# One transposed order of q's halves, and the other made by two VectorE copies

## Chip, core and metric

The kernel runs on one core of a Trainium2 chip. The metric is the device time of one execution in microseconds; of several runs the median is taken.

## What is computed

An attention layer is followed by two feed-forward layers. The change touches only the attention's preparation of q. Cut to that part, the reference is:

```python
q_pool = q.reshape(B, H, S // 2, 2, D).mean(axis=3)      # B 4, H 8, S 1152, D 64
scores = (1 / np.sqrt(D)) * np.matmul(q_pool, k.transpose(0, 1, 3, 2))
attn = softmax(scores)                                   # 1e-09 added to the sum
x = np.matmul(attn, v)                                   # then moe 1 (h * cos(h)), moe 2 (silu)
```

All inputs are float32.

## The kernel before

TensorE multiplies in float16, so each float32 operand is scaled and split into two float16 halves, hi and lo, and products of halves are summed in PSUM.

**Pairs.** The 32 heads are worked through as 16 pairs. Per pair `pair_loads` (L429) loads q, k and v through SyncE's queue (L433, L436, L442); `pair_prep` (L453) adds the two rows of q that are pooled (POOL, L456), takes absolute maxima (VectorE, `absmax` L126), makes the scales (`scale_steps`, L111 to L119) and splits q (L489 to L495), k (`split`, L446 and L451) and v (`do_v`).

**q and k.** The head dimension is 64, so two halves fit on 128 rows. k's hi and lo are laid side by side and transposed by one DMA (L507): rows 0 to 63 of kT are hi, rows 64 to 127 lo. q is made in two orders, e = 0 as hi over lo and e = 1 as lo over hi. ScalarE casts hi twice (L491), VectorE makes lo once (L492, a fused multiply and subtract) and copies it once (L495), and one DMA transposes both orders, 2 x 9 blocks of 128 x 128 (L497). `tile_scores` (L518) multiplies kT with qT of e = 0 and then of e = 1 into the same PSUM tile, which gives all four products of halves.

**Tiles.** A pair has 9 tiles of 128 query rows. Each tile passes TensorE (scores, L531 or L539), VectorE (scale and minimum out of PSUM, L550, L555), ScalarE (exp, L558; hi cast, L564), POOL (lo, L569), a DMA transpose of 18 blocks (L571) and TensorE again (product with v, L582 and L586). The scores have one PSUM buffer for each of their two column parts. `LAG` keeps four tiles between scores and the product with v.

**Order.** Python generators emit the work: while pair n's tiles run, `prep_then_load` (L957) emits the preparation of pair n + 1 and the loads of pair n + 2, one step every few calls (`slowly`). In the first four pairs the weights of layer 1 are prepared beside this; from the fifth on, matmuls of layer 1 (L667, L722) are mixed in. A scheduler then puts all instructions into one fixed order for each engine's queue by their place in the program, with an offset where `ahead` is used, as they come ready in its own timeline. On the chip each queue runs strictly in that order; an instruction whose input isn't there holds all behind it. All DMAs here, loads and transposes alike, are issued from SyncE's queue (SP).

**Buffers.** qn and kn share the tag "kn" with two buffers (`NB_N`), so qn is always in the one and kn in the other.

Of the kernel before, what the change touches and what calls it, by code (L numbers as in the profile page):

```python
# [12 lines left out]
F16 = mybir.dt.float16  # L13
I32 = mybir.dt.int32
AF = mybir.ActivationFunctionType
ALU = mybir.AluOpType
# [8 lines left out]
END = object()  # L25
P_CH, P_SC, P_EX, P_PV, P_MS, P_MU, P_W, P_PR, P_X = 0, 60, 0, -100, 200, 0, 0, 0, 0
PSH = 15.0
NB_N, NB_SC, NB_H, NB_T, NB_S = 2, 4, 4, 4, 5
X_LAG = 40
W1_BUFS, WT_BUFS = 3, 3  # L30
W1_TABLE = (6, (0, 2, 4, 8, 11), 2)
# [17 lines left out]
def attention_moe_moe_kernel(ctx, tc, q, k, v, w_in1, w_out1, w_in2, w_out2, out):  # L49
# [3 lines left out]
    nc = tc.nc  # L53
    B, H, S, D = q.shape
# [4 lines left out]
    KC = S // 128  # L59
# [24 lines left out]
    def scale_steps(m, pool, res, top, wide=False, apart=False, clean=False, put=lambda ins: ins):  # L84

        n = m.shape[1]
        if wide:  # L90
            w = small.tile([128, 1], F32, name="mw", tag="mw")
            wi, mi = w.bitcast(I32), m.bitcast(I32)
            put(nc.vector.tensor_scalar(
                out=wi, in0=mi, scalar1=3, scalar2=EXP_MASK if clean else 0x3F800000, op0=ALU.logical_shift_left,
                op1=ALU.bitwise_and
            ))
            if not clean:
                nc.vector.scalar_tensor_tensor(
                    out=wi, in0=mi, scalar=1 << 30, in1=wi, op0=ALU.bitwise_and, op1=ALU.bitwise_or
                )  # L100
            m = w
            if apart:
                yield
        if pool is ps_y:
            bc = pool.tile([128, NC, GW], F32, tag="y", name="bm")[:, 0, 0:4]
        else:
            bc = pool.tile([128, 2, GW], F32, tag="h", name="bm")[:, 0, 0:4]
        put(nc.tensor.matmul(bc[:, 0:n], mean, m, start=True, stop=True))
        yield
        s, u = res  # L110
        nc.vector.tensor_scalar(  # L111
            out=u, in0=bc[:, 0:n], scalar1=TINY, scalar2=2.0**(9 - top), op0=ALU.max, op1=ALU.mult
        )

        nc.vector.tensor_scalar(
            out=s.bitcast(I32), in0=u.bitcast(I32), scalar1=EXP_MASK, scalar2=EXP_MASK,
            op0=ALU.bitwise_and, op1=ALU.bitwise_xor,
        )
        nc.vector.tensor_scalar(  # L119
            out=u.bitcast(I32), in0=u.bitcast(I32), scalar1=EXP_MASK, scalar2=None, op0=ALU.bitwise_and  # L120
        )
# [3 lines left out]
    def absmax(out_, in_, axis=AX.X):  # L125
        nc.vector.tensor_reduce(out=out_, in_=in_, axis=axis, op=ALU.max, apply_absolute_value=True)  # L126
# [9 lines left out]
    def early(g, n):  # L136
        while True:
            with ahead(n):
                r = next(g, END)
            if r is END:  # L140
                return
            yield r
# [264 lines left out]
    def att_pools(stack):  # L407
        at = Weights()
        at.p = stack.enter_context(tc.tile_pool(name="att", bufs=2, side="right", reuse_waits="tile"))
        at.src_stack = ExitStack()  # L410
        at.src = at.src_stack.enter_context(tc.tile_pool(name="src", bufs=2, side="right", reuse_waits="tile"))
        at.ps_s = stack.enter_context(tc.tile_pool(name="ps_s", bufs=1, space=PSUM, side="right"))
        at.ps_v = stack.enter_context(tc.tile_pool(name="ps_v", bufs=1, space=PSUM, side="right"))
        return at
# [30 lines left out]
    def split(hi, lo, src, s, on_pool):  # L445
        nc.scalar.activation(out=hi, in_=src, func=AF.Copy, scale=s)  # L446
        if on_pool:
            nc.scalar.activation(out=src, in_=src, func=AF.Copy, scale=s)
            nc.gpsimd.tensor_tensor(out=lo, in0=src, in1=hi, op=ALU.subtract)
        else:  # L450
            nc.vector.scalar_tensor_tensor(out=lo, in0=src, scalar=s, in1=hi, op0=ALU.mult, op1=ALU.subtract)  # L451

    def pair_prep(at, P):  # L453
        NQ = 2 * NT + 1
        qs = P.q[:, :, 0, :]
        nc.gpsimd.tensor_tensor(out=qs, in0=qs, in1=P.q[:, :, 1, :], op=ALU.add)  # L456
        m = small.tile([128, 5], F32, name="pm", tag="pm")
        for i in range(2):
            absmax(m[:, 1 + i:2 + i], P.k[i], AX.XY)
            yield  # L460
        absmax(m[:, 0:1], qs, AX.XY)
        yield
        for i in range(2):
            absmax(m[:, 3 + i:4 + i], P.v[i], AX.XY)
            yield
        m3 = small.tile([128, 3], F32, name="pm3", tag="pm3")
        nc.vector.tensor_copy(m3[:, 0:1], m[:, 0:1])
        nc.vector.tensor_reduce(
            out=m3[:, 1:3], in_=m[:, 1:5].rearrange("p (a b) -> p a b", b=2), axis=AX.X, op=ALU.max
        )  # L470
        s = small.tile([128, 3], F32, name="ps_", tag="ps_", bufs=3)
        u = small.tile([128, 3], F32, name="pu_", tag="pu_", bufs=3)
        yield from early(scale_steps(m3, ps_h, (s, u), 12), P_CH)
        P.s = s
        P.su = small.tile([128, 1], F32, name="psu", tag="psu", bufs=3)
        nc.vector.tensor_scalar(
            out=P.su, in0=u[:, 0:1], scalar1=u[:, 1:2], scalar2=-0.125 / math.sqrt(D), op0=ALU.mult, op1=ALU.mult
        )
        P.vt = [None] * 2

        def do_v(i):

            P.vt[i] = vt = at.p.tile([128, KC, 2, D + 1], F16, tag="vt", name="vt", bufs=VT_BUFS)
            nc.gpsimd.memset(vt[:, :, 0, D:D + 1], 1.0)
            nc.gpsimd.memset(vt[:, :, 1, D:D + 1], 0.0)
            split(vt[:, :, 0, 0:D], vt[:, :, 1, 0:D], P.v[i], s[:, 2:3], P.on_pool >= 2)


        qn = at.src.tile([128, 2, NQ, 2, D], F16, tag="kn", name="qn", bufs=NB_N)  # L489
        for e in range(2):  # L490
            nc.scalar.activation(out=qn[:, e, :, e, :], in_=qs, func=AF.Copy, scale=s[:, 0:1])  # L491
        nc.vector.scalar_tensor_tensor(  # L492
            out=qn[:, 0, :, 1, :], in0=qs, scalar=s[:, 0:1], in1=qn[:, 0, :, 0, :], op0=ALU.mult, op1=ALU.subtract
        )
        nc.vector.tensor_copy(qn[:, 1, :, 0, :], qn[:, 0, :, 1, :])  # L495
        qT = at.p.tile([128, 2, NQ, 128], F16, tag="qT", name="qT", bufs=2)
        nc.sync.dma_start_transpose(  # L497
            out=qT.rearrange("p e n k -> p (e n) k"), in_=qn.rearrange("p e n s d -> p (e n s d)")
        )
        P.qT = [qT[:, e] for e in range(2)]  # L500
        yield
        kn = at.src.tile([128, 2, KC, 2, D], F16, tag="kn", name="kn", bufs=NB_N)
        for i in range(2):
            split(kn[:, i, :, 0, :], kn[:, i, :, 1, :], P.k[i], s[:, 1:2], P.on_pool >= 1)
            yield
        kT = at.p.tile([128, 2, KC, 128], F16, tag="kT", name="kT", bufs=2)
        nc.sync.dma_start_transpose(  # L507
            out=kT.rearrange("p i c k -> p (i c) k"), in_=kn.rearrange("p i c s d -> p (i c s d)")
        )
        P.kT = [kT[:, i].rearrange("p c k -> p (c k)") for i in range(2)]  # L510
        yield
        for i in range(2):
            do_v(i)
            yield
# [348 lines left out]
    if True:  # L863
# [6 lines left out]
        at = att_pools(att_stack)  # L870
# [69 lines left out]
        for n in range(2):  # L940
            P[n] = pair_new(at, *pairs[n])
            run_all(pair_loads(P[n]))
            if n == 0:
                wg = layer1_weight_steps(W1, (w_in1, w_out1), wst, lambda: ps_y, nc.sync, W1_BUFS, WT_BUFS, *W1_TABLE)
                next(wg)
                run_all(pair_prep(at, P[0]))
                next(wg)
# [9 lines left out]
        def prep_then_load(n):  # L957
            late = int(n > NP)
            yield from early(slowly(pair_prep(at, P[n]), PREP_PACE[late]), P_PR)
            if n + 1 < len(pairs):  # L960
                P[n + 1] = pair_new(at, *pairs[n + 1])
                yield from slowly(pair_loads(P[n + 1]), LD_PACE[late])
# [290 lines left out]
```

## Time and profile before

| | |
|---|---|
| median of 3 runs | 1365.03 us (1364.72 to 1366.87) |
| the profiled execution's own time | 1363.93 us |
| its span, first to last instruction | 1362.1 us |
| mean granted TensorE clock | 0.925 of full speed |
| busy TensorE, VectorE, ScalarE, POOL | 1139.0, 1039.7, 870.9, 620.3 us |
| DMA queue q1, share of 16 engines' span | 65.8% |
| DMA transposes: hl, q, k, x, x rest | 144, 16, 16, 8, 2 |

Attention runs until about 836 us and overlaps with layer 1 from about 257 us on; the rest is layers 1 and 2. "Busy" is the time with an instruction in work, and a wait is put down to whatever came last. SP's rows give the time for which its queue was issuing a DMA; "to landing" is counted from the start of the issue to the last byte.

### The profile page before, as it was taken

Reading aid. Unit: us, or ns where it says so; the run is one execution under the profiler, and the core shown is the slowest. Engines: PE = TensorE matmul, PEld = TensorE weight load, DVE = VectorE, ACT = ScalarE, POOL = GpSimd, SP = SyncE. Lnnn points to the kernel's source line nnn. Section 1 sums busy time; section 2 is a strip of 40 time slices with the busy share of each in tenths; the row PEclk is TensorE's granted clock in tenths of the full one; section 3 lists DMA queues with packets and bytes.
Section 4 is the critical chain, followed back from the end, with each engine's and each line's share of the span. In section 5 each row is a group of like instructions: output and inputs, shape, how many; then the busy total and the mean of one; then the engine's idle time right before and its main releaser. Section 6 shows DMA issues by size and latency. Waiting matters only on the chain. (4 is left out here: it accounts for less than half of the span.)

```text
span 1362.1 us, 26442 instructions
## 1 busy us (share of the span) xinstructions
PE 1139.0 (84%) x10668; PEld 915.3 (67%) x10668; DVE 1039.7 (76%) x1927; ACT 870.9 (64%) x1061; POOL 620.3 (46%) x352
## 2 busy tenths in 40 slices
PE   2565465788988777889898899989999999999998
PEld 1343243576666556666676678778788888888887
DVE  6898888789876988888898996886757755444483
ACT  3878787778767777877788774544546633433352
POOL 1656675666556466656556562443667400000000
PEclk9667676889998889999899999999899999999999
DMA  9999999988799999988999965423444000000001
GB/s 290 202 212 226 221 231 183 163 168 166 135 204 177 201 199 198 198 151 186 157 202 188 217 129 109 106 81 71 86 91 112 32 25 32 9 16 17 17 32 32
DMA packets 509594, 186.27 MB, mean 137 GB/s; under 512 B 465952, under 2 KB 484384, under 8 KB 509472
## 3 DMA queue, kind: packets, MB, share of 16 engines
q1 hardware_dynamic: 509472, 184.59, 65.8%
q8 instruction: 83, 1.36, 0.4%
q14 instruction: 39, 0.32, 0.1%
HBM read 66.58 MB, written 9.44 MB: 56 GB/s over the span
## 5 line engine op out<-in xcount | busy, mean ns | idle before, releaser
L569 POOL TENSOR_TENSOR hl<-sc,hl 128x1152 f16<-128x1152 f32 x144 | 367.9, 2565 | 201.2 <-ACT hl L564 105.9
L531 PE MATMUL sp<-kT,qT 128*128 128x512 f16 (+1 forms) x768 | 189.4, 366 | 92.7 <-DVE sc L550 70.8
L550 DVE TENSOR_SCALAR_CACHE_REDUCE sc<-sp,psu 128x512 f32<-128x512 f32 (+1 forms) x288 | 228.9, 807 | 49.6 <-PE sp L531 46.2
L667 PEld LDWEIGHTS <-ih 128*128 128x128 f16 x2304 | 225.5, 99 | 42.9 <-issue 12.4
L558 ACT ACTIVATE sc<-sc,nb 128x1152 f32<-128x1152 f32 x144 | 179.8, 1250 | 114.4 <-DVE nb L555 77.8
L582 PE MATMUL pv<-vt,hlT 128*128 128x130 f16 (+1 forms) x1440 | 195.1, 237 | 65.9 <-DMA hlT<-hl 58.3
L582 PEld LDWEIGHTS <-hlT 128*128 128x128 f16 (+1 forms) x1440 | 146.4, 110 | 96.1 <-DMA hlT<-hl 73.4
L667 PE MATMUL h<-ys,ih 128*128 128x256 f16 x1152 | 195.5, 274 | 4.1 <-ACT gs L683 4.1
L667 PE MATMUL h<-xT,ih 128*128 128x256 f16 x1024 | 184.9, 275 | 3.2 <-DMA xT<-xn 3.1
L586 PE MATMUL pv<-vt,hlT 128*128 128x65 f16 (+1 forms) x1440 | 186.3, 207 | 0.0
L531 PEld LDWEIGHTS <-qT 128*128 128x128 f16 x768 | 76.9, 108 | 156.9 <-issue 104.2
L564 ACT ACTIVATE hl<-sc 128x1152 f16<-128x1152 f32 x144 | 164.6, 1153 | 14.5 <-DMA xT<-xn 9.7
L722 PE MATMUL y<-gh,oh 128*128 128x256 f16 x576 | 162.0, 281 | 7.1 <-ACT y L731 7.1
L722 PE MATMUL y<-gl,oh 128*128 128x256 f16 x576 | 161.8, 281 | 2.9 <-POOL gl L711 2.9
L722 PE MATMUL y<-gh,ol 128*128 128x256 f16 x576 | 161.8, 281 | 0.0
L836 PEld LDWEIGHTS <-op 128*128 128x128 f16 x1512 | 147.9, 98 | 18.0 <-issue 0.6
L667 PE MATMUL h<-ys,il 128*128 128x256 f16 x576 | 157.7, 274 | 0.0
L586 PEld LDWEIGHTS <-hlT 128*128 128x128 f16 (+1 forms) x1440 | 143.0, 108 | 15.8 <-issue 6.1
L667 PE MATMUL h<-xT,il 128*128 128x256 f16 x512 | 140.5, 274 | 0.0
L722 PEld LDWEIGHTS <-oh 128*128 128x128 f16 x1152 | 114.8, 102 | 28.1 <-issue 9.4
L711 POOL TENSOR_TENSOR gl<-tt,gh 128x1024 f16<-128x1024 f32 x36 | 92.1, 2559 | 76.4 <-DVE gh L710 71.2
L667 PEld LDWEIGHTS <-il 128*128 128x128 f16 x1152 | 113.7, 99 | 17.8 <-issue 2.9
(310 smaller groups left out, 2039.9 us busy)
## 6 DMA issues: line engine op xcount, KB each, us to landing
wst<-in_moe_w_in_dram SPq DMA_DIRECT2D x16, 1024.0 KB, 5.8
stk<-in_k_dram SPq DMA_DIRECT2D x32, 288.0 KB, 4.0
stv<-in_v_dram SPq DMA_DIRECT2D x32, 288.0 KB, 4.0
stq<-in_q_dram SPq DMA_DIRECT2D x32, 256.0 KB, 3.1
wst<-in_moe_w_out_dram SPq DMA_DIRECT2D x8, 1024.0 KB, 6.2
wst<-in_moe_w_out_dram SPq DMA_DIRECT2D x16, 512.0 KB, 6.0
ydr<-y SPq DMA_DIRECT2D x9, 512.0 KB, 4.3
y32b<-ydr SPq DMA_DIRECT2D x9, 512.0 KB, 3.3
```

The costliest lines, as they stand in the source:

```text
L531: nc.tensor.matmul(sp[:, o - a:o - a + n], P.qT[e][:, t, :], kT[:, o:o + n], start=(e == 0), stop=(e == 1))
L550: nc.vector.tensor_scalar(out=T.sc[:, a:z], in0=sp, scalar1=T.P.su, scalar2=None, op0=ALU.mult, op1=ALU.min, accum_out=mx[:, x:x + 1],)
L558: nc.scalar.activation(out=T.sc, in_=T.sc, func=AF.Exp, scale=-1.0, bias=nb)
L564: nc.scalar.activation(out=hi, in_=T.sc, func=AF.Copy)
L569: nc.gpsimd.tensor_tensor(out=T.hl[:, 1, :], in0=T.sc, in1=T.hl[:, 0, :], op=ALU.subtract)
L582: nc.tensor.matmul(G.pv[r, T.gi], T.hlT[:, 0, c, r], P.vt[i][:, c], start=(c == 0), stop=(c == KC - 1), skip_group_check=True,)
L586: nc.tensor.matmul(G.pv[r, T.gi, 0], T.hlT[:, 1, c, r], P.vt[i][:, c, 0], start=False, stop=(c == KC - 1), skip_group_check=True,)
L667: nc.tensor.matmul(hp, wt[:, c, f * 128:(f + 1) * 128], xt(c), start=(i == 0), stop=(i == 3 * NC - 1), skip_group_check=True,)
L711: nc.gpsimd.tensor_tensor(out=G.gl, in0=t, in1=gh, op=ALU.subtract)
L722: nc.tensor.matmul(blk.y[:, oc, :], wt[:, f, oc * 128:(oc + 1) * 128], gt[:, f % 4, :], start=(f == 0 and e == 0 and oc % 2 == 0), stop=(f ...
L836: nc.tensor.matmul(bank, t[:, e, c, :], wt[:, c, :], start=start, stop=True, skip_group_check=True)
```

## The change

q is split once, hi beside lo, into a buffer of half the size with a tag of its own (one buffer; kn too now has one). The DMA transposes 9 blocks into e = 0 of qT. After the transpose of k has been issued, two VectorE copies write e = 1: rows 0 to 63 from rows 64 to 127 of e = 0, and rows 64 to 127 from rows 0 to 63.

```diff
-        qn = at.src.tile([128, 2, NQ, 2, D], F16, tag="kn", name="qn", bufs=NB_N)
-        for e in range(2):
-            nc.scalar.activation(out=qn[:, e, :, e, :], in_=qs, func=AF.Copy, scale=s[:, 0:1])
-        nc.vector.scalar_tensor_tensor(
-            out=qn[:, 0, :, 1, :], in0=qs, scalar=s[:, 0:1], in1=qn[:, 0, :, 0, :], op0=ALU.mult, op1=ALU.subtract
-        )
-        nc.vector.tensor_copy(qn[:, 1, :, 0, :], qn[:, 0, :, 1, :])
+        qn = at.src.tile([128, NQ, 2, D], F16, tag="qn", name="qn", bufs=1)
+        split(qn[:, :, 0, :], qn[:, :, 1, :], qs, s[:, 0:1], False)
         qT = at.p.tile([128, 2, NQ, 128], F16, tag="qT", name="qT", bufs=2)
-        nc.sync.dma_start_transpose(
-            out=qT.rearrange("p e n k -> p (e n) k"), in_=qn.rearrange("p e n s d -> p (e n s d)")
-        )
+        nc.sync.dma_start_transpose(out=qT[:, 0], in_=qn.rearrange("p n s d -> p (n s d)"))
         P.qT = [qT[:, e] for e in range(2)]
         yield
-        kn = at.src.tile([128, 2, KC, 2, D], F16, tag="kn", name="kn", bufs=NB_N)
+        kn = at.src.tile([128, 2, KC, 2, D], F16, tag="kn", name="kn", bufs=1)
...
         P.kT = [kT[:, i].rearrange("p c k -> p (c k)") for i in range(2)]
+        for x, y in ((slice(0, 64), slice(64, 128)), (slice(64, 128), slice(0, 64))):
+            nc.vector.tensor_copy(qT[x, 1], qT[y, 0])
         yield
```

## Rows read from the trace of the kernel before

**Rows 1.** Busy us of PE, PEld, DVE, ACT, POOL by stage; clock, DMA share, GB/s.
```profile
0.00:267.00 267.00, 144.64 (x1190) 95.44 (x1191) 224.09 (x501) 197.70 (x220) 154.54 (x91) 0.74 1.01 219
267.00:500.00 233.00, 192.28 (x1927) 145.55 (x1925) 193.22 (x384) 174.89 (x208) 138.87 (x74) 0.93 0.94 176
500.00:850.00 350.00, 311.05 (x3137) 239.43 (x3136) 303.80 (x587) 265.08 (x320) 201.40 (x103) 0.98 0.90 174
```

**Rows 2.** Who waited for whom: us in total, times, longest us.
```profile
PE sp L531 <- DVE sc L550: 70.8, 56, 8.6
...
PE pv L582 <- DMA hlT<-hl: 58.3, 30, 5.6
...
DVE pm L126 <- DMA stk<-in_k_dram: 23.4, 13, 6.3
...
DVE pm L126 <- DMA stv<-in_v_dram: 7.0, 5, 2.3
```

**Rows 3.** Timeline of the first pair: start us, us, engine, line; idle before it.
```profile
9.35 0.14 DVE L467 COPY pm<-pm 128x1 f32<-128x1 f32 x1
...
13.43 1.44 ACT L491 ACTIVATE qn<-stq,ps__150 128x576 f16<-128x576 f32 x2
14.24 0.82 DVE L492 SCALAR_TENSOR_TENSOR qn<-stq,ps__150,qn 128x576 f16<-128x576 f32 x1 [1.72 <-ACT qn L491]
...
15.57 1.55 DVE L451 SCALAR_TENSOR_TENSOR kn<-stk,ps__150,kn 128x576 f16<-128x576 f32 x2 [0.15 <-ACT kn L446]
15.67 3.95 SPq L497 DMA_TRANSPOSE qT<-qn  x1
...
19.73 2.75 SPq L507 DMA_TRANSPOSE kT<-kn  x1
...
24.33 2.08 PE L531 MATMUL sp<-kT,qT 128*128 128x512 f16 x6 [12.66 <-DMA kT<-kn]
```

**Rows 4.** Tile qn and tile qT: count, ns shortest, median, longest, starts; time to landing.
```profile
L495 DVE COPY qn<-qn x16: 310/319/781, 15.1 to 748.7; 128x576 f16<-128x576 f16 x16
L497 SPq DMA_TRANSPOSE qT<-qn x16: 2680/3202/5333, 15.7 to 749.1; - x16
...
L492 DVE SCALAR_TENSOR_TENSOR qn<-stq,ps__7680,qn x1: 2924/2924/2924, 653.0 to 653.0; 128x576 f16<-128x576 f32 x1
...
DMA to landing us min/median/max: 4.6/5.8/7.5
```

**Rows 5.** Page, queue q1 (packets, MB, share of 16 DMA engines) and memory totals.
```profile
q1 hardware_dynamic: 509472, 184.59, 65.8%
...
HBM read 66.58 MB, written 9.44 MB: 56 GB/s over the span
```

**Rows 6.** Columns as in rows 1, for a stretch with plain transfers only.
```profile
1000.00:1362.00 362.00, 352.88 (x3213) 314.36 (x3210) 202.86 (x307) 161.42 (x228) 52.86 (x48) 1.00 0.12 35
```

**Rows 7.** Tile xrT, transposes of 8 blocks: ns in SP's queue, us to landing.
```profile
L1097 SPq DMA_TRANSPOSE xrT<-xnr x2: 1355/1491/1627, 876.8 to 879.1; - x2
...
DMA to landing us min/median/max: 3.6/4.3/5.1
```

**Rows 8.** Line L710 by itself: ns shortest, median, longest.
```profile
L710 DVE CAST gh<-tt x36: 665/686/2856, 269.2 to 988.0; 128x1024 f16<-128x1024 f32 x36
```

**Rows 9.** Groups by line and shape: busy us, mean ns, idle before them.
```profile
L569 POOL TENSOR_TENSOR hl<-sc,hl 128x1152 f16<-128x1152 f32 x144 | 367.9, 2565 | 201.2 <-ACT hl L564 105.9 <-issue 45.9 <-DVE sc L550 12.1
...
L710 DVE CAST gh<-tt 128x1024 f16<-128x1024 f32 x36 | 46.0, 1277 | 2.1 <-PE y L722 2.0
```

**Rows 10.** Timeline of the fifth pair, columns as in rows 3.
```profile
217.54 2.21 DVE L492 SCALAR_TENSOR_TENSOR qn<-stq,ps__1893,qn 128x576 f16<-128x576 f32 x1
...
221.30 2.71 SPq L507 DMA_TRANSPOSE kT<-kn  x1
224.10 2.74 SPq L497 DMA_TRANSPOSE qT<-qn  x1
...
228.81 2.99 PE L531 MATMUL sp<-kT,qT 128*128 128x512 f16 x8 [6.07 <-DMA qT<-qn]
```

More of the change, by code (lines that the diff above doesn't have):

```diff
@@ L27 @@
 PSH = 15.0
-NB_N, NB_SC, NB_H, NB_T, NB_S = 2, 4, 4, 4, 5
+NB_SC, NB_H, NB_T, NB_S = 4, 4, 4, 5
 X_LAG = 40
```

## The prediction

> **What bounds the kernel now.** I read the busy times by stage first. Attention fills the time up to about 850 us, and there no engine is full: VectorE is busy 224.1 + 193.2 + 303.8 = 721.1 of 850 us (85%), TensorE 648.0 (76%), while the DMA engines' share is 1.01, 0.94 and 0.90 [rows 1]. In the first stage TensorE works 144.6 of 267 us at a mean granted clock of 0.74, so part of that time at the lower of its two levels (1.2 and 2.4 GHz). After 850 us TensorE is nearly always at work [rows 6] and the change touches nothing. So the change is worth what it does to TensorE's 850 - 648.0 = 202.0 idle us before that. The table of waits comes next: 70.8 us of them end with VectorE's reading of the scores' PSUM (35%), 58.3 us with the landing of a tile's transpose hlT (29%) [rows 2]. I use these two shares as prices: a microsecond added to VectorE's queue costs 0.35, one taken off the chain ScalarE, POOL, DMA that ends in hlT gives back 0.29. That is a choice: a share of waits says what ended them last, not what would end them next.
>
> **What goes: ScalarE.** Two casts in a row take 1.44 us [rows 3], so one takes 0.72; 16 pairs, 11.5 us. It stands in front of the exps and hi casts that feed hlT: 11.5 x 0.29 = 3.3 us.
>
> **What goes: half a transpose.** Queue q1 holds the 16 engines for 65.8% of 1362.1 = 896 us and moves 184.6 MB, of which 76.0 MB are reads and writes of memory [rows 5]. In the stretch without transposes 0.12 x 362 = 43.4 us moved 35 GB/s x 362 us = 12.7 MB, 3.43 us per MB [rows 6]. So plain transfers hold 261 us and the 186 transposes 635 us, an estimated 3.4 us each. Half of q's is 1.7 us a pair, 27.3 us over 16. SP's queue gains as well: q's issue takes 3.20 us at the median [rows 4], 8 blocks take 1.36 to 1.63 [rows 7], so 9 should take some 1.6. The queue behind it is that of the tiles' hlT, so both go to the same wait: 27.3 x 0.29 = 7.9 us. Ends: nothing, if no hlT ever stood behind a q transpose, and the full 1.7 in those pairs where the DMA is full.
>
> **What comes: two VectorE copies a pair.** Each covers 64 rows x 1152 float16. No row shows a copy between halves of the partitions. The nearest is the removed copy, the same type and engine, 576 elements in 310 ns at the shortest [rows 4]; a one-element copy takes 140 ns [rows 3]; so 0.295 ns an element and 0.14 + 0.34 = 0.48 us for 1152. Upper end: the cast from float32, (665 - 140) / 1024 = 0.513 ns an element [rows 8], 0.73 us. Lower end: 0.31, as the removed one. I take 0.48, since type and memory are the same; two are 0.96 us. The removed copy gives back 0.32.
>
> Copies also wait for POOL. The cast L710 takes 0.665 us at the shortest and 1.277 on average, up to 2.86 [rows 8, 9], and q's own subtract 0.82 us alone and 2.92 beside POOL [rows 3, 4]. I take the cast's 1.277 - 0.665 = 0.61 us, once a pair, as the second copy follows the first. The Trainium skill (SBUF — State Buffer, "two separate sides") speaks against the change here: POOL and a VectorE copy use one pair of ports, whoever starts first keeps it for a whole instruction, and the other stands still. By that rule the wait would be POOL's busy share times half of one of its instructions; rows 1 and 9 give 495 / 850 x 2.565 / 2 = 0.75 us, and the sum would be 0.8 us higher. The trace agrees in kind (2.92 for 0.82), and the measured 0.61 stays in the sum.
>
> Together 0.96 + 0.61 - 0.32 = 1.25 us a pair, 20.0 us of VectorE.
>
> **A new wait.** The copies wait for qT's landing, on VectorE's queue, where the next tile's L550 stands behind them, and TensorE's next scores wait for L550. Before, only TensorE waited for qT, usually long after. Landing takes 5.8 us now [rows 4]; for 8 blocks 4.3 [rows 7]. How much of it shows depends on what the fixed order puts between. The nearest row of VectorE waiting for a DMA in its queue is the absolute maxima on k and v: 30.4 us over 64 loads [rows 2], 0.48 us a transfer, or 1.9 us for the four of a pair. I take 0.48 (one transfer), 7.6 us in all; ends 0 and 1.9 us a pair. VectorE in all: 27.6 x 0.35 = 9.7 us lost.
>
> **What moves on SP.** qT's issue no longer waits for the copy L495 and is shorter. In the first pair kT is issued at 19.73, right after q's 3.95 us, though kn was ready at 15.57 + 1.55 = 17.12; the scores start at 24.33 when kT lands [rows 3]. q's issue would start at about 15.1 (14.24 + 0.82) and take 2.0, so kT goes at 17.1, 2.6 us earlier. The copies must be done too: 15.1 + 4.3 = 19.4, two copies 20.4, and a subtract of 0.82 us or the like that VectorE has begun may come first. The scores could start near 22: I take 2.0 us, ends 0 and 2.6. In the fifth pair qn's lo ends at 219.75, kT goes at 221.30 and qT only at 224.10, and TensorE waits 6.07 us for it until 228.81 [rows 10]. Without L495 qT can go first and land near 224; then kT's landing and the copies come last, near 226: I take 2.0 us, ends 0 and 3.5. For the other pairs I count nothing: they are prepared while the tiles of the pair before still run, and that work hides an earlier landing.
>
> The smaller qn in a buffer of its own adds no wait: it is written once in some 50 us, long after its transpose. kn had one buffer in effect before, and has one now.
>
> **The sum.** -2.0 (first pair) -2.0 (fifth) -7.9 (DMA and SP) -3.3 (ScalarE) +9.7 (VectorE) = -5.5 us. The profiled execution took 1363.93 us, of which the span is 1362.1; so it would take 1358.4. The median of the runs stands 1.1 us above the profiled one: 1365.03 - 5.5 = 1359.5 us. With the ends of the copies, of the wait and of the two starts the same sum runs from about 1353 to 1374.
>
> **Rivals.**
> *VectorE stalls behind q's transpose (slower).* Place: the first copy, with L550 behind it. For it: VectorE runs in order, SP's queue lags (qT was issued 4 us after it could have been in the fifth pair, rows 10). Against: VectorE has q's, k's and v's subtracts to do meanwhile. Price: a wait that happened was 30.4 / 18 = 1.69 us [rows 2], and it passes in full, since TensorE's scores wait behind. The rest of the sum without the 7.6 us is -15.2 + 20.0 x 0.35 = -8.2, so it decides from five pairs on; ten of sixteen give +8.7, 1373.7 us; all sixteen 1383.8.
> *POOL holds up both copies (slower).* Each copy waits half a POOL instruction, 1.28 us: 41.0 us in place of 9.8, so +5.4 in all, 1370.4 us. For it: the rows of L710. Against: the removed copy's median of 319 ns.
> *It cancels.* If VectorE's microseconds cost 0.55 instead of 0.35, the 27.6 us are 15.2 and the sum is nought: 1365.0 us. For it: VectorE is the busiest engine up to 267 us, at 84%.
> *The DMA is the bound of the first stage (much faster).* Share 1.01 there: five pairs get the full 1.7 us (8.6), the other eleven 0.29 of it (5.5), 14.1 in place of 7.9, 1353.3 us. Against: hlT's landing ends only 29% of TensorE's idle time.
> That the change doesn't do what it says I leave out: the swapped halves are exactly the other order.
>
> **How the numbers follow.** A measurement of this kernel can tell about 0.2%, 2.7 us, from no change. Forecast 0.38 (of which 0.32 beyond that, 0.06 within), DMA bound 0.12, cancelling 0.18, stall 0.24, POOL 0.08. So faster 0.44, same 0.24, slower 0.32. Cases of both signs hold most of it; the range goes from 1350, below the DMA case, to 1374, and leaves out the stall in more than ten pairs.
>
> **What would show it.** Right: kT's issue near 17 and first scores near 22 us; no wait for qT in the fifth pair; q's issue at 1.5 to 2 us; 32 copies of 0.5 us shortest; fewer waits of L582 for hlT. Wrong: VectorE's wait for qT at the new copies above 1 us a pair, or copies of 0.7 us shortest and 1.3 on average; the DMA share unchanged; TensorE's idle time before 850 us at 202 us or above.

## The result

| | before | changed |
|---|---|---|
| median | 1364.88 us | 1382.45 us |
| lowest to highest of 4 runs | 1363.76 to 1366.87 | 1379.84 to 1387.84 |
| span of the profiled execution | 1362.1 us | 1378.0 us |
| busy VectorE, ScalarE | 1039.7, 870.9 us | 1069.9, 861.2 us |

The change makes the kernel slower: ratio 1.0121, 95% interval 1.0093 to 1.0150, 17.6 us at the medians. 1359.5 was predicted, with 1374 as the upper end. The last product with v starts at 852.7 us in the changed kernel and at 835.8 us before, so nearly all of the loss arises in attention.

The stages of the changed kernel, with the columns of [rows 1]:

```profile
0.00:267.00 267.00, 141.88 (x1155) 91.91 (x1156) 241.73 (x502) 194.55 (x214) 158.28 (x91) 0.76 0.95 211
267.00:500.00 233.00, 194.50 (x1903) 146.15 (x1901) 192.38 (x377) 167.17 (x196) 132.27 (x73) 0.93 0.89 168
500.00:850.00 350.00, 304.21 (x3031) 228.75 (x3030) 310.16 (x578) 260.66 (x313) 205.79 (x104) 0.97 0.87 169
```

The DMA engines' share fell in every stage, as was meant. VectorE's busy time up to 850 us rose by 23.2 us, to 744.3 (88%), and TensorE got 7.4 us less done in the same time. The waits answer to [rows 2]:

```profile
ACT sc L553 <- DVE nb L550: 113.2, 51, 9.5
...
PE sp L526 <- DVE sc L545: 90.7, 69, 5.7
...
PE pv L577 <- DMA hlT<-hl: 30.8, 19, 5.5
```

The first of these lines in the kernel before:

```profile
ACT sc L558 <- DVE nb L555: 77.8, 40, 8.1
```

TensorE's waits for a tile's transpose nearly halved, by 27.5 us. Its waits for VectorE's reading of the scores rose by 19.9 us on the same line, and ScalarE's exps now wait 113.2 us for VectorE's minimum, where they waited 77.8. The waits for a transpose were replaced by waits for VectorE. The lines of q's preparation answer to [rows 4]:

```profile
L505 DVE COPY qT<-qT x32: 454/455/2539, 23.6 to 766.6; 64x1152 f16<-64x1152 f16 x32
L492 SPq DMA_TRANSPOSE qT<-qn x16: 1242/1300/2165, 15.2 to 759.9; - x16
...
DMA to landing us min/median/max: 3.2/3.4/6.3
```

The transpose is cheap as hoped: 1.30 us in SP's queue for 3.20, landing after 3.4 us for 5.8. A copy takes 0.455 us, but up to 2.5. Their group (busy us, mean ns, idle before):

```profile
L505 DVE COPY qT<-qT 64x1152 f16<-64x1152 f16 x32 | 28.5, 890 | 0.7
```

The mean is 0.890, so of the 28.5 us 14.6 are work (32 x 0.455) and 13.9 are not; and VectorE stood idle in front of the copies for only 0.7 us in all, so it didn't wait for q's transpose. The timeline of the second pair shows what the 13.9 us are (start us, us, engine, line):

```profile
46.08 2.13 POOL L226 TENSOR_TENSOR il<-wt,ih 128x1024 f16<-128x1024 f32 x1 [1.69 <-ACT wt L225]
...
46.69 4.39 DVE L505 COPY qT<-qT 64x1152 f16<-64x1152 f16 x2
...
48.17 2.60 POOL L564 TENSOR_TENSOR hl<-sc,hl 128x1152 f16<-128x1152 f32 x1
51.11 0.75 DVE L545 TENSOR_SCALAR_CACHE_REDUCE sc<-sp,psu 128x512 f32<-128x512 f32 x1
...
51.92 0.59 PE L526 MATMUL sp<-kT,qT 128*128 128x512 f16 x1 [4.51 <-DVE sc L545]
```

Two copies take 4.39 us instead of 0.91: POOL is in one instruction when they begin and in the next before they end. L545 of the next tile comes only after them, and TensorE waits 4.51 us for it. In the whole trace the 13.9 us lie in ten of the 32 copies, every one of them beside a POOL instruction; they belong to seven of the 16 pairs, and in three of these both copies waited.

### The profile page after: what moved, and what is told of

It is laid out like the page before. It is cut to its first block, busy times and chain, and to the rows that moved or that the text cites. A ratio compares the mean times of both kernels' runs of the same rounds, so it can differ in the third digit from the quotient of the medians.

```text
span 1378.0 us, 26428 instructions
## 1 busy us (share of the span) xinstructions
PE 1146.5 (83%) x10668; PEld 916.1 (66%) x10668; DVE 1069.9 (78%) x1943; ACT 861.2 (62%) x1045; POOL 627.0 (45%) x352
## 3 DMA queue, kind: packets, MB, share of 16 engines
q1 hardware_dynamic: 491040, 179.87, 62.5%
## 5 line engine op out<-in xcount | busy, mean ns | idle before, releaser
L564 POOL TENSOR_TENSOR hl<-sc,hl 128x1152 f16<-128x1152 f32 x144 | 372.5, 2595 | 205.8 <-ACT hl L559 111.9
L526 PE MATMUL sp<-kT,qT 128*128 128x512 f16 (+1 forms) x768 | 193.2, 365 | 103.4 <-DVE sc L545 90.7
L553 ACT ACTIVATE sc<-sc,nb 128x1152 f32<-128x1152 f32 x144 | 179.8, 1251 | 135.9 <-DVE nb L550 113.2
L662 PEld LDWEIGHTS <-ih 128*128 128x128 f16 x2304 | 226.5, 100 | 44.0 <-issue 11.5
L545 DVE TENSOR_SCALAR_CACHE_REDUCE sc<-sp,psu 128x512 f32<-128x512 f32 (+1 forms) x288 | 228.0, 806 | 34.0 <-PE sp L526 29.7
L577 PE MATMUL pv<-vt,hlT 128*128 128x130 f16 (+1 forms) x1440 | 199.3, 238 | 44.7 <-DMA hlT<-hl 30.8
L662 PE MATMUL h<-xT,ih 128*128 128x256 f16 x1024 | 193.0, 280 | 1.5 <-DMA xT<-xn 1.5
L581 PE MATMUL pv<-vt,hlT 128*128 128x65 f16 (+1 forms) x1440 | 190.5, 208 | 0.0
L662 PE MATMUL h<-xT,il 128*128 128x256 f16 x512 | 143.3, 280 | 0.0
L717 PEld LDWEIGHTS <-oh 128*128 128x128 f16 x1152 | 113.7, 100 | 30.2 <-issue 12.4
```

Of the source, the lines that this page charges most:

```text
L526: nc.tensor.matmul(sp[:, o - a:o - a + n], P.qT[e][:, t, :], kT[:, o:o + n], start=(e == 0), stop=(e == 1))
L545: nc.vector.tensor_scalar(out=T.sc[:, a:z], in0=sp, scalar1=T.P.su, scalar2=None, op0=ALU.mult, op1=ALU.min, accum_out=mx[:, x:x + 1],)
L553: nc.scalar.activation(out=T.sc, in_=T.sc, func=AF.Exp, scale=-1.0, bias=nb)
L564: nc.gpsimd.tensor_tensor(out=T.hl[:, 1, :], in0=T.sc, in1=T.hl[:, 0, :], op=ALU.subtract)
L577: nc.tensor.matmul(G.pv[r, T.gi], T.hlT[:, 0, c, r], P.vt[i][:, c], start=(c == 0), stop=(c == KC - 1), skip_group_check=True,)
L581: nc.tensor.matmul(G.pv[r, T.gi, 0], T.hlT[:, 1, c, r], P.vt[i][:, c, 0], start=False, stop=(c == KC - 1), skip_group_check=True,)
```

## The experiments

The theories, as they came up. **A**: VectorE's added time is the loss, whatever fills it. **B**: the new fixed order of the queues is the loss. **C** and **D**: the wait for q's transpose is (C on the scores' path, D on VectorE's queue). **L**: only standing behind POOL is. **X**: crossing the halves of the partitions is. All times below are medians; the ratio is to the kernel before on the same chip, with its 95% interval, and can differ by some 0.002 from the quotient of the medians. Each kernel gets a fixed order of its own.

### What is the halved transpose worth without the copies?

```diff
-        P.qT = [qT[:, e] for e in range(2)]
+        P.qT = [qT[:, 0], qT[:, 0]]
...
-        for x, y in ((slice(0, 64), slice(64, 128)), (slice(64, 128), slice(0, 64))):
-            nc.vector.tensor_copy(qT[x, 1], qT[y, 0])
```

> The changed kernel without the two VectorE copies; the second matmul of each score reads the same order as the first, so those products are wrong but as many. Theory A (VectorE's load: the copies' 28.5 us on VectorE are the loss, the halved transpose and the cast give a little back): faster than before, 1350 to 1362 us. Theory B (the new fixed order of instructions is the loss, whatever is in it): near the changed kernel, 1374 to 1385. Theory C (the copies make the scores wait for q's transpose and VectorE): as A.

Measured: 1367.92 us, ratio 0.9990 (0.9967 to 1.0014). The half transpose, the cast and L495 are gone, nothing is added, and the time doesn't move. Its waits:

```profile
PE sp L524 <- DVE sc L543: 93.5, 65, 4.8
...
PE pv L575 <- DMA hlT<-hl: 38.0, 27, 5.1
```

Here too the waits for hlT fell (58.3 to 38.0), and those for VectorE rose by as much (70.8 to 93.5), with no work added on VectorE. So, by the interval, the relief is worth between a gain of 4.5 us and a loss of 1.9. The prediction had 11.2 for it, and 4.0 more for the two earlier starts. Unless a loss by order hides a gain here, which this run alone can't exclude (theory B), the whole loss of the change comes with the copies.

### The copies added to the kernel before

```diff
         P.kT = [kT[:, i].rearrange("p c k -> p (c k)") for i in range(2)]
+        for x, y in ((slice(0, 64), slice(64, 128)), (slice(64, 128), slice(0, 64))):
+            nc.vector.tensor_copy(qT[x, 1], qT[y, 0])
```

> The kernel before, all its casts and its whole transpose kept, with the two copies added at the place where the change has them; they write again the values that are there. Theory A: the loss of the change plus what it gave back, 1383 to 1395 us. Theory B: anywhere from 1360 to 1385, not above the changed kernel for a reason. Theory C: at least the changed kernel, 1380 to 1395.

Measured: 1384.45 us, ratio 1.0106 (1.0071 to 1.0140). The copies alone bring the loss of the whole change. Their load isn't the same, though: they take 42.0 us here for 28.5, and VectorE waits 9.2 us for q's transpose in front of them:

```profile
L512 DVE COPY qT<-qT 64x1152 f16<-64x1152 f16 x32 | 42.0, 1313 | 9.7 <-DMA qT<-qn 9.2
```

Within the interval nothing is given back by the halved transpose, as in the run without copies.

### Copies of two columns

In the changed kernel:

```diff
-        P.qT = [qT[:, e] for e in range(2)]
+        P.qT = [qT[:, 0], qT[:, 0]]
...
-            nc.vector.tensor_copy(qT[x, 1], qT[y, 0])
+            nc.vector.tensor_copy(qT[x, 1, 0, 0:2], qT[y, 0, 0, 0:2])
```

> The changed kernel with each copy cut to two columns, so that the wait for the transpose and the place in VectorE's queue stay and the load goes; the second matmul reads the first order as in the run without copies. Theory A: as without copies, within 4 us, 1350 to 1362. Theory B: near the changed kernel, 1374 to 1385. Theory C (the wait itself): 1372 to 1385, while the run without copies is fast.

Measured: 1381.20 us, ratio 1.0094 (1.0057 to 1.0131). And in the kernel before, into a scratch tile:

```diff
         P.kT = [kT[:, i].rearrange("p c k -> p (c k)") for i in range(2)]
+        qx = at.src.tile([128, 2], F16, tag="qx", name="qx", bufs=1)
+        for x, y in ((slice(0, 64), slice(64, 128)), (slice(64, 128), slice(0, 64))):
+            nc.vector.tensor_copy(qx[x], qT[y, 0, 0, 0:2])
```

> The kernel before with two copies of two columns from q's transpose into a scratch tile that nobody reads: a new wait on VectorE and a new fixed order, nearly no load. Theory A: 1362 to 1369 us. Theory B: it differs from before by 5 us or more, either way. Theory C: 1370 or more.

Measured: 1380.60 us, ratio 1.0090 (1.0061 to 1.0119). Both lose nearly as much as the full copies, and theory A as I had put it looked dead. But the load had not gone. The group of the second kernel:

```profile
L513 DVE COPY qx<-qT 64x2 f16<-64x2 f16 x32 | 24.1, 754 | 4.6 <-DMA qT<-qn 4.1
```

A copy of two columns takes 754 ns on average (567 in the other kernel), where 165 is the shortest. The timeline of one pair:

```profile
49.93 2.38 POOL L572 TENSOR_TENSOR hl<-sc,hl 128x1152 f16<-128x1152 f32 x1
50.41 2.12 DVE L513 COPY qx<-qT 64x2 f16<-64x2 f16 x2 [0.91 <-DMA qT<-qn]
```

POOL's instruction ends at 52.31, and two copies that need 0.3 us end at 52.53. So what a copy costs here hardly depends on its length, and these kernels carry 24.1 and 18.1 us on VectorE for 28.5.

### Order alone

Two memsets of two columns at the same place (kernel before):

```diff
         P.kT = [kT[:, i].rearrange("p c k -> p (c k)") for i in range(2)]
+        qx = at.src.tile([128, 2], F16, tag="qx", name="qx", bufs=1)
+        for x in (slice(0, 64), slice(64, 128)):
+            nc.vector.memset(qx[x], 0.0)
```

> The kernel before with two memsets of two columns a pair on VectorE, at the place in the program where the change has its copies: no load to speak of, no wait for q's transpose, but another fixed order (about 1320 of VectorE's 1609 instructions keep their relative place). Theory B (a new fixed order costs about 1%, whatever made it new): 1372 to 1386 us. Theory D (a VectorE instruction that waits for q's transpose is what costs): 1363 to 1370.

Measured: 1369.08 us, ratio 1.0010 (0.9995 to 1.0024).

```diff
-LD_PACE = (2, 2)
+LD_PACE = (2, 3)
```

In the kernel before:

> The kernel before with the loads of later pairs emitted one call later (LD_PACE (2, 3) for (2, 2)): the same instructions, another fixed order from the fifth pair on. Theory B: the order of before is a good draw, this one is 1368 to 1385 us. Theory D: 1362 to 1370.

Measured: 1370.17 us, ratio 1.0013 (0.9997 to 1.0028). In the changed kernel:

> The changed kernel with the same other pace of loads. Theory B: another draw, anywhere from 1365 to 1390 us, at least 4 us from the changed kernel. Theory D: 1378 to 1386, as the changed kernel, since the copies still wait.

Measured: 1384.34 us, ratio 1.0117 (1.0082 to 1.0151). Three new orders, and none moves its kernel by more than 0.2%. That makes theory B unlikely as the cause of 1.2%; an order can still be worth some tenths of a per cent, and one kernel below loses 1% without any work added on VectorE.

### Covering the wait

```diff
-        for x, y in ((slice(0, 64), slice(64, 128)), (slice(64, 128), slice(0, 64))):
-            nc.vector.tensor_copy(qT[x, 1], qT[y, 0])
...
         for i in range(2):
             do_v(i)
             yield
+        for x, y in ((slice(0, 64), slice(64, 128)), (slice(64, 128), slice(0, 64))):
+            nc.vector.tensor_copy(qT[x, 1], qT[y, 0])
+        yield
```

> The changed kernel with the two copies emitted as the last step of a pair's preparation, behind v's split, so that the transpose has long landed. Theory B: 1374 to 1388 us, as the changed kernel. Theory D: the wait is covered, 1362 to 1372.

Measured: 1381.98 us, ratio 1.0094 (1.0069 to 1.0120). The later place gives nothing back, as there was hardly a wait to cover. To take the wait away altogether, the two-column copies read qn, which is there before q's transpose is issued (kernel before):

```diff
+            nc.vector.tensor_copy(qx[x], qn[y, 0, 0, 0, 0:2])
```

> The kernel before with two two-column copies between halves of the partitions a pair, but from qn, which is ready before q's transpose is issued, so nothing waits for the transpose. Theory L: means of 0.4 to 0.8 us for copies of 0.17 at the shortest, 1374 to 1386 us. Theory D: 1363 to 1372.

Measured: 1390.40 us, ratio 1.0159 (1.0125 to 1.0192). No wait for the transpose, and the loss is larger, with 13.6 us of copies on VectorE. The opposite, the wait without a copy:

```diff
+            nc.vector.tensor_reduce(out=qx[x], in_=qT[y, 0, 0, 0:2], axis=AX.X, op=ALU.max)
```

> The run with two-column copies on the kernel before (1380.6 us), with each copy turned into a maximum over the same two columns (a tensor_reduce): the same wait for q's transpose, the same place, an operation whose longest duration in the trace of before shows no wait for POOL. Theory L (a VectorE copy stands still while POOL is in an instruction, however short it is): shortest and mean duration nearly equal, 1363 to 1372 us. Theory D (the wait for q's transpose costs): 1376 to 1386.

Measured: 1375.01 us, ratio 1.0046 (1.0023 to 1.0068), between the two expectations.

```profile
L513 DVE TENSOR_REDUCE qx<-qT x32: 150/152/154, 25.4 to 775.6; 64x1 f16<-64x2 f16 x32
```

The maximum never stands behind POOL (150 to 154 ns, where the copy had 165 to 2417), and VectorE's wait for the transpose was 4.5 us in all. Half a per cent remains that may be this wait or the order. It may also be time of VectorE: its busy time as a whole rose from 1039.7 to 1060.9 us, though the maxima are only 4.9 us of that, so other instructions of it took longer. With the run from qn, theories C and D fall as the main cause.

### Crossing the halves

```diff
+        for x in (slice(0, 64), slice(64, 128)):
+            nc.vector.tensor_copy(qx[x], qT[x, 0, 0, 0:2])
```

> The kernel before with two two-column copies a pair that stay on their own rows (rows 0 to 63 to 0 to 63, 64 to 127 to 64 to 127). Theory L (the copy stands behind POOL): as with crossing rows, mean 0.4 to 0.8 us for 0.17 at the shortest, 1374 to 1386 us. Theory X (crossing the halves of the partitions is what costs): 1363 to 1371.

Measured: 1381.00 us, ratio 1.0095 (1.0069 to 1.0121), mean 735 ns. Copies that stay on their rows cost what crossing ones cost: X falls.

### The copies off VectorE

```diff
-            nc.vector.tensor_copy(qT[x, 1], qT[y, 0])
+            nc.scalar.activation(out=qT[x, 1], in_=qT[y, 0], func=AF.Copy)
```

> The changed kernel with the two copies on ScalarE in place of VectorE, about 1.2 us each, 38 us in all against 11.5 us saved there. Theory L: no wait for POOL; ScalarE has room, 1360 to 1376 us. Theory D (any engine's wait for q's transpose): 1376 to 1390.

Measured: 1369.87 us, ratio 1.0014 (0.9991 to 1.0038), with copies of 1.16 us each, never longer. ScalarE takes 37 us of copies nearly for nothing where VectorE couldn't take 28.5.

```diff
-            nc.vector.tensor_copy(qT[x, 1], qT[y, 0])
+            nc.sync.dma_start(out=qT[x, 1], in_=qT[y, 0])
```

> The changed kernel with the two copies as plain DMAs on SP's queue, 147 KB each: no engine works for them, but SP's queue stands until q's transpose has landed, and half of the saved DMA time is spent again. Theory L: about as without copies, 1358 to 1372 us. Theory D: the tiles' transposes behind them are late, 1374 to 1390.

Measured: 1368.37 us, ratio 0.9996 (0.9978 to 1.0015). With the same two lines moved up behind q's transpose:

> The copies as DMAs on SP's queue, emitted right behind q's transpose instead of behind k's: the waits of TensorE for the copied order (10.2 us in the run with DMAs) go, kT may be later. 1357 to 1368 us if that is what kept that run from gaining; 1366 to 1374 if SP's standing is paid by kT.

Measured: 1367.94 us, ratio 1.0000 (0.9983 to 1.0018). With `nc.scalar.dma_start` at the change's own place:

> The changed kernel with the two copies as plain DMAs from ScalarE's queue, so that SP's queue doesn't stand for the landing; ScalarE may. Could beat the kernel before if the halved transpose is worth anything: 1357 to 1370 us. If it is worth nothing, 1364 to 1370; if ScalarE stands, 1370 or more.

Measured: 1382.11 us, ratio 1.0101 (1.0078 to 1.0123), the one run without work on VectorE that loses 1%. That is above the first two ranges, and the third case isn't what happened: the trace shows no wait of ScalarE for q's transpose. Its DMA issues (us to landing last):

```profile
hlT<-hl SPq DMA_TRANSPOSE x144, 5.3
...
kT<-kn SPq DMA_TRANSPOSE x16, 6.3
```

The tiles' transposes land after 5.3 us (4.9 in the run without copies) and k's after 6.3 (4.8), and ScalarE's queue issues 32 DMAs of 0.5 us. Which of these costs, or whether it is the order, wasn't tried. None of the three forms beats the kernel before.

### Time or POOL

```diff
-            nc.vector.tensor_copy(qT[x, 1], qT[y, 0])
+            nc.vector.tensor_reduce(
+                out=qT[x, 1], in_=qT[y, 0].rearrange("p n (k o) -> p n k o", o=1), axis=AX.X, op=ALU.max
+            )
```

> The changed kernel with each copy made by a maximum over one element (a tensor_reduce of 64 x 1152), which should take about 1.34 us each time (estimate from the absolute maxima, 0.74 us for 576 elements), 43 us in all against 28.5 for the copies, and never stand behind POOL. Theory L: faster than the changed kernel, 1366 to 1378 us. Theory A (VectorE's busy time alone, at the 17.5 us for 30 that the change shows): slower than it, 1386 to 1396.

Measured: 1384.09 us, ratio 1.0121 (1.0090 to 1.0151), 1.346 to 1.349 us each, 43.1 us in all. It lies between the two expectations, below A's too. Never behind POOL, and the same loss as the copies: L alone is not it. The last two runs add only instructions that wait neither for POOL nor for the transpose (kernel before):

```diff
         P.kT = [kT[:, i].rearrange("p c k -> p (c k)") for i in range(2)]
+        qx = at.src.tile([128, 1], F16, tag="qx", name="qx", bufs=1)
+        for x, y in ((slice(0, 64), slice(64, 128)), (slice(64, 128), slice(0, 64))):
+            nc.vector.tensor_reduce(out=qx[x], in_=qn[y, 0, :, 0, :], axis=AX.XY, op=ALU.max)
```

> The kernel before with two maxima of 64 x 576 elements of qn a pair on VectorE into a scratch tile: 0.74 us each (estimate from the absolute maxima on k), 24 us in all, the time that the tiny copies took, with no wait for q's transpose and none for POOL. Theory A (VectorE's time is what costs, whatever fills it): 1377 to 1386 us, as the tiny copies. Theory L (only standing behind POOL costs): 1363 to 1371.

Measured: 1387.63 us, ratio 1.0155 (1.0121 to 1.0188), a little above A's range. With `in_=qn[y, 0].rearrange("p n s d -> p (n s) d")`:

> The same with 64 x 1152 elements, 1.34 us each, 43 us in all. Theory A: 1385 to 1400 us, above the run with 576 elements. Theory L: 1363 to 1371.

Measured: 1397.51 us, ratio 1.0225 (1.0195 to 1.0256). The groups of the two kernels:

```profile
L513 DVE TENSOR_REDUCE qx<-qn 64x1 f16<-64x576 f16 x32 | 24.0, 750 | 0.7
```

```profile
L513 DVE TENSOR_REDUCE qx<-qn 64x1 f16<-64x1152 f16 x32 | 43.2, 1350 | 0.7
```

Theory A is the one that is left, though the loss isn't in proportion (see the end). Against 1366.71 us for the kernel before on that chip, 24.0 us of maxima cost 20.9 (0.87 each) and 43.2 cost 30.8 (0.71 each). The added instructions aren't all that VectorE had more to do: its busy time as a whole rose by 43.3 us (1039.7 to 1083.0) and 62.7 us (to 1102.4), since others of its instructions took longer too (the copy L495 alone 10.1 us for 5.6 in the first of the two). A new order alone moved this total by -6.5 us (other pace) and +3.2 (memsets). By these totals a microsecond cost 0.48 and 0.49, and in the change 17.6 / 30.2 = 0.58 (1039.7 to 1069.9). Why the others took longer wasn't tried.

## Why the prediction was wrong

**Two steps failed, and both are prices.** I took shares of TensorE's waits for what a microsecond is worth. From the forecast -5.5 us to the measured +17.6 are 23.1 us. If the relief is put at nought, as the run without copies has it, 15.2 of them are relief that didn't come (7.9 for the DMA, 3.3 for ScalarE, 4.0 for the two starts), and 7.9 are VectorE's term, 17.6 for 9.7. With VectorE's price alone put right the sum would have been -15.2 + 17.6 = +2.4 us, within 0.2% of no change.

**The price of VectorE's time.** I took 0.35, the share of TensorE's waits that VectorE ended. The runs that add only maxima measured 0.87 and 0.71 per microsecond added (0.48 and 0.49 of VectorE's total). The change puts 28.5 us of copies on VectorE and takes away the removed copy's 5.6 (16 x 347 ns, their mean in the kernel before, 319 at the median [rows 4]), 22.9 net; at 0.71 to 0.87 that is 16 to 20 us, and 17.6 were lost. The amount was below my 27.6. That these two prices meet the loss so well is in part luck: reckoned in the same way, the full copies in the kernel before cost 17.4 / 42.0 = 0.41, and the two-column copies from qn 23.3 / 13.6 = 1.71.

**The price for ScalarE and the DMA, 0.29.** What these two were relieved of was much as forecast: ScalarE 9.7 us of work for 11.5, the DMA engines 35 us for 27.3 (896 us before; queue q1's share of 62.5% of 1378.0 us is 861), and the waits for hlT fell. But the run without copies shows at most 4.5 us for it, and most likely none. TensorE's idle time is a sum over waits in which several things are late; take one away and the next one, VectorE, is there. A share of the waits is no price, in either direction. That VectorE's price is so much above 0.35 because it is 85 to 88% busy, and because its queue holds each tile's L545 in front of TensorE and ScalarE, is argued, not shown.

**Point by point.**
- Length of a copy: 0.455 us for 0.48. Right.
- Waiting for POOL: 13.9 us for 9.8. I had counted one wait a pair, "as the second copy follows the first"; the second pair's timeline has POOL's next instruction in between. By the rule of the Trainium skill (SBUF — State Buffer, "two separate sides") I had 0.75 us a pair for my 0.61, and 13.9 / 16 = 0.87 was measured. The trace agrees with the rule in kind: every copy that took longer lay beside a POOL instruction. That the size comes so near is in part luck: seven pairs of 16 waited, 2.0 us each, where that reckoning had 0.58 of them (POOL's busy share) and 1.28 us.
- VectorE's wait for q's transpose: 0.7 us idle before the copies, for 7.6. The rival that the copies stall there is wrong, and covering the wait changed nothing.
- First pair: kT was issued at 17.45 and the scores began at 22.16, as forecast. But the copies came at 23.58, behind other work of VectorE, and the matmuls of the second order, which need them, stood until 24.56. The start at 24.33 [rows 3] was beaten by 2.2 us and nothing came of it: the next tile's scores began at 27.75 us, and at 27.30 before. The changed kernel's rows:

```profile
17.45 3.30 SPq L500 DMA_TRANSPOSE kT<-kn  x1
...
22.16 1.01 PE L526 MATMUL sp<-kT,qT 128*128 128x512 f16 x2 [10.39 <-DMA kT<-kn]
...
23.58 0.92 DVE L505 COPY qT<-qT 64x1152 f16<-64x1152 f16 x2
...
24.56 1.25 PE L526 MATMUL sp<-kT,qT 128*128 128x512 f16 x4 [1.39 <-DVE qT L505]
```

- Fifth pair: TensorE's only wait for q's transpose is now the first pair's; the 6.07 us [rows 10] are gone, and the total shows nothing of it.
- The rival with POOL came nearest in kind: half of the copies' time is spent behind POOL. But it had 41.0 us of waiting for the 13.9, and its 1370.4 us rest on the same prices. The stall in all sixteen pairs had 1383.8 us, close to the measured time, by a wait that isn't there: luck.
- TensorE's idle time before 850 us is 850 - 640.6 = 209.4 us, above 202, as my signs of being wrong had it.
- The sum with the measured prices, made afterwards: 22.9 x 0.79 (the middle of the two) = +18.1, and nought for the rest, 1383.0 us for 1382.45. As other runs give other prices, it proves little.

**What stays open.** The loss isn't in proportion to VectorE's time in every kernel: 13.6 us of copies from qn lost 23.3 us, the copies as maxima, 43.1 - 5.6 = 37.5 us net, only 17.0. Eight kernels with 12 to 43 us more on VectorE (net of L495 where it goes) lost 0.9 to 2.3% beside the change itself and its other pace and place; of the eight with less, six stayed within 0.2%, and two did not (1.0046, 1.0101). Each has its own order, and how much of a single figure is due to that can't be told from these runs.

## What to carry to other kernels

A share of the waits tells what came last, not what a saved microsecond is worth: put a known load on the engine in question (here two maxima a pair) and measure its price before moving work to it. Where TensorE, VectorE and ScalarE are each busy for 75 to 88% of the time, as here, work belongs on the one whose added time is cheap, whatever its own duration: ScalarE took copies of 1.16 us nearly for nothing where VectorE's of 0.455 cost 1.2%. A short VectorE copy beside a busy POOL cost here by whether it met one of POOL's instructions, hardly by its length.

## What was not expected of the hardware

- A VectorE copy of 64 x 2 float16 between the halves took 165 ns at the shortest and 2417 at the longest, 426 to 754 on average over three kernels beside POOL's work; a maximum over the same columns took 150 to 154 ns each time.
- A copy between halves of the partitions runs at the rate of one in place: 454 ns for 64 x 1152 float16, 0.27 ns an element above the 140 ns of a one-element copy [rows 3], where the removed copy had 0.295 [rows 4].
- A DMA transpose of 9 blocks took 1.30 us in SP's queue and 3.4 us to land, less than the 4.3 us of 8 blocks that I had gone by [rows 7], of which there were only two.
